# A tile of the input is made 128 bytes wider, and every tile behind it in SBUF moves by 128 bytes

## The chip, the core and the metric

The kernel runs on one core of a Trainium2 chip. The metric is device time in microseconds (us) of one execution. The core has five engines that run side by side: TensorE (PE in the profile, its weight loads PEld), VectorE (DVE), ScalarE (ACT), GpSimd (POOL) and SyncE (SP), which here issues nearly all the DMAs. Tiles lie in SBUF, 128 partitions wide. A tile has the same start address in each partition, and "offset" below is that address modulo 512 bytes.

## What is computed

Tokens (2 sequences of 4096, 192 wide) pass a causal convolution of 7 taps whose weights are a softmax per head, then a gated layer, then a second layer with ELU:

```python
w = softmax(weight)                                  # 8 heads x 7 taps
x = einsum('hk,bskhg->bshg', w, unfold(x))           # (8192, 192)
gate = 1.0 / (1.0 + np.exp(-(x @ w_gate)))           # 192 -> 1536
x = (gate * (x @ w_val)) @ w_out                     # 1536 -> 192
h = x @ w_in                                         # 192 -> 2048
g = np.where(h > 0.0, h, np.exp(np.minimum(h, 0.0)) - 1.0)
return g @ w_out2                                    # 2048 -> 192
```

## The kernel before

The 8192 tokens are cut into 16 blocks of 512 (`TB`). Each float32 operand of a product is split into a high and a low part (`h`, `l`, type fp32r), and a product is the sum of three matmuls: high by high, low by high, high by low. All large matmuls come from one helper, `mm` on L294: 64 partitions of weights by 128 columns, times 64 partitions by 512 tokens. They stand in pairs, one for the lower 64 partitions and one for the upper (`HALVES`), and each one has a weight load of its own.

- `front` (L294 with output `ps`) makes one 128-wide piece of a layer's hidden width from the block's tiles `xn`, `xs`, `xr` (the first 128 rows, the same with its halves exchanged, and the remaining 64 rows held twice). Weights: `w1h`, `w1l` in the first layer, `w3h`, `w3l` in the second.
- ACT and DVE evaluate the gate or the ELU (L311, L313, L323 to L327), ACT copies the result to `gh` (L334), and DVE writes the rest into `gl` (L340).
- `back` (L294 with output `a`) multiplies `gh` and `gl` with `w2s` or `w4s`, two steps later (`LAG`).
- `exchange` (L150, L151) makes `xs` from `xn` by two DMAs within SBUF. `end1` and `end2` fold the sums into the next layer's `xn`, `xs`, `xr` or write the output; their `three` is made from `two` by DMA (L399, L400, L445).
- `load_x` (L153) fetches a block of x from HBM into a tile `x0` or `x1`, 518 floats wide: 512 tokens and 6 before them (`PAD`). `conv` makes the convolution from it, on TensorE for two of its parts (L172, weights in the tiles `gh` and `gl`, whole 128 partitions, float32), on DVE for the others (L179, L183).
- Weights come from HBM as 64-bit numbers in the first 200 us and are split by `narrow` into the resident tiles.

The order of the work is written out by hand: a list of steps, with `CONV`, `PREPARED` and `at` to say at which step a piece of side work is issued. The changed line touches none of these.

Where tiles lie. SBUF is given out pool by pool, in the order in which the pools are opened, and within a pool in the order in which its tiles are first asked for; each tile is rounded up to 32 bytes. The built program of before has these addresses (bytes within a partition):

| tiles | first address | offset in 512 | read by matmuls as |
|---|---|---|---|
| `w1h`, `w1l`, `w3h`, `w3l`, `w2s`, `w4s` | 16,512 to 96,384 | 128, all of them | weights, in pieces of 512 bytes |
| `x0`, two buffers | 148,896 and 150,976 | 416 and 448 | moving operand of L172 |
| `x1`, one buffer | 153,056 | 480 | moving operand of L172 |
| `xcv`, `xn`, `xs`, `xr` | 155,136 to 192,000 | 0 | moving operand of `front` |
| `g`, `e`, `gh`, `gl`, `one`, `two` | 196,096 to 226,816 | 0 | `gh`, `gl`: moving operand of `back`, weights of L172 |

Of the kernel before, what the change touches and what calls it, by code (L numbers as in the profile page):

```python
# [8 lines left out]
F32 = mybir.dt.float32  # L9
# [11 lines left out]
P = 128  # L21
DR = D - P
TB = 512
NB = B * S // TB
PAD = TAPS - 1
# [33 lines left out]
def conv_glu_elu_kernel(  # L59
# [23 lines left out]
    xin = ctx.enter_context(tc.tile_pool(name="xin", bufs=2))  # L83
# [53 lines left out]
    xin_t = {}  # L137
# [14 lines left out]

    def load_x(b, i):  # L153

        t = xin_t[b, i] = xin.tile([P, TB + PAD], F32, tag=f"x{i}", name=f"x{i}", bufs=2 - i)
        if i == 0:
            bi, t0 = divmod(b * TB, S)
            nc.sync.dma_start(t, xp[0:P, bi, t0:t0 + TB + PAD])
        else:
            for h in range(2):  # L160
                bi, t0 = divmod((b + h) * TB, S)
                (nc.sync if b else nc.scalar).dma_start(t[DR * h:DR * (h + 1)], xp[P:D, bi, t0:t0 + TB + PAD])
        yield

    def conv(b, i):


        x = xin_t[b, i]
        if (b, i) in diagonals:
            acc = ps_w.tile([P, TB], F32, tag="w", name="ps")  # L170
            for k, w in enumerate(diagonals[b, i]):
                nc.tensor.matmul(acc, w, x[:, k:k + TB], start=k == 0, stop=k == TAPS - 1)  # L172
            yield
        else:
            acc = xcv.tile([P, TB], F32, tag=f"xcv{i}", name="xcv")
            for k in range(TAPS):
                w, xk = cwn[:, i, k:k + 1], x[:, k:k + TB]
                if k:
                    nc.vector.scalar_tensor_tensor(acc, xk, w, acc, ALU.mult, ALU.add)  # L179
                elif b == 2:  # L180
                    nc.scalar.mul(acc, xk, w)
                else:
                    nc.vector.tensor_scalar_mul(acc, xk, w)  # L183
                yield

        for blocks in ([0], [1]) if i and b == 2 else ([0, 1], ) if i else ([0], ):
            rows = [slice(DR * n, DR * (n + 1)) if i else slice(0, P) for n in blocks]
            made = [parts(1, b + n, "nr"[i]) for n in blocks]
            for (h, l), r in zip(made, rows):
                nc.scalar.copy(h[r], acc[r])  # L190
            yield
            for (h, l), r in zip(made, rows):
                nc.vector.tensor_sub(l[r], acc[r], f32(h[r]))
            if i == 0:
                exchange(1, b)
            yield
            if i:
                for n, r in zip(blocks, rows):
                    t = f32(parts_t[1, b + n]["r"])
                    nc.sync.dma_start(t[DR * (1 - n):DR * (2 - n)], t[r])  # L200
                yield
# [279 lines left out]
    with tc.manual_schedule():  # L481
# [28 lines left out]

        nc.sync.dma_start(cws, cw)
        next(load_x(0, 0))
        next(load_x(0, 1))
        next(jobs[0])
        next(load_x(1, 0))
        next(jobs[1])
        next(jobs[2])
# [34 lines left out]
        for (b, i), pieces in CONV.items():  # L552
            f = conv(b, i)
# [8 lines left out]
        for i in range(int(min(extra)) - 1, len(steps) + LAG + 2):  # L562
# [3 lines left out]
            if past and past[0][1] < 2:  # L566
                kind, b, j = past[0]
                past = [(kind, n, j) for n in range(2)] if b else []
            if now:
                kind, b, j = now  # L570
# [77 lines left out]
```

## Time and profile before

| | |
|---|---|
| Time, median of 3 runs | 1227.03 us (1226.5 to 1228.39) |
| Span of the profiled execution, first to last instruction | 1224.6 us |
| PE busy | 1215.9 us, 99% |
| PEld busy | 1037.0 us, 85% |
| DVE, ACT, POOL busy | 848.6, 791.3, 77.0 us |
| Granted TensorE clock | 9 (90% or more) in all 40 slices |

The page gives engine totals first, then the span in slices, then the chain of work that ended last. A matmul's own duration in the trace is its time from start to the end of its drain, which overlaps the next one; what a stream of matmuls costs is read from the distance between starts. "Pair" below means the two matmuls of the two halves, which start within some nanoseconds of each other in most of the trace.

### The profile page before, as it was taken

The numbers are of one execution on the slowest core, as the hardware profiler recorded it, in microseconds if no ns is written. First come the engines' busy times: TensorE is split into PE (matmuls) and PEld (weight loads), VectorE is DVE, ScalarE is ACT, GpSimd is POOL, SyncE is SP. The second block draws the span as 40 slices with busy tenths as digits, with TensorE's granted clock in tenths as the row PEclk, the third lists the DMA queues.
The fourth block names the chain that finished last, engine by engine and source line by source line (L and its number), as shares of the span: only waits on it lengthen the run. The fifth ranks groups of instructions, "written<-read, shape, count | busy, mean of one in ns | idle before, by whom it ended". The sixth has DMA issues, their size and how long they took to land.

```text
span 1224.6 us, 24965 instructions
## 1 busy us (share of the span) xinstructions
PE 1215.9 (99%) x10276; PEld 1037.0 (85%) x10276; DVE 848.6 (69%) x1288; ACT 791.3 (65%) x1376; POOL 77.0 (6%) x66
## 2 busy tenths in 40 slices
PE   9999999999999999999999999999999999999998
PEld 5889999888888888887888899999888888888886
DVE  8997698785447876577666676666766667664565
ACT  5555788854448885448854488445884468844686
POOL 0000000101001000011001010010100100001010
PEclk9999999999999999999999999999999999999999
DMA  6655340311001020111112011020110201111100
GB/s 156 220 194 177 104 134 27 87 53 44 9 19 44 18 61 20 31 30 45 29 34 56 7 44 45 18 61 1 44 44 19 61 11 35 44 35 27 27 14 18
DMA packets 31954, 65.78 MB, mean 54 GB/s; under 512 B 4512, under 2 KB 15776, under 8 KB 31840
## 3 DMA queue, kind: packets, MB, share of 16 engines
q1 hardware_dynamic: 31680, 63.92, 18.7%
q8 instruction: 80, 1.31, 0.4%
q10 hardware_dynamic: 160, 0.27, 0.1%
q14 instruction: 34, 0.28, 0.1%
HBM read 19.74 MB, written 6.29 MB: 21 GB/s over the span
## 4 chain that ended last, share of the span: by engine, by line
PE 92%; DVE 3%; ACT 2%; issue 1%; DMA 1%; SPq 1%; ACTq 0%; DVEq 0%
PE ps L294 51%; PE a L294 41%; DMA s<-in_w_dram 1%; ACT e L324 0%; DVE g L327 0%; ACT e L323 0%; SPq L216 0%; DVE gl L340 0%; ACT gh L334 0%; DVE h L249 0%; DVE g L313 0%; ACT gh L133 0%; DVE xcv L179 0%; ACT t L236 0%; DVE t L243 0%
## 5 line engine op out<-in xcount | busy, mean ns | idle before, releaser
L334 ACT CAST gh<-g 128x512 fp32r<-128x512 f32 x448 | 273.7, 618 | 187.7 <-DVE g L313 145.8
L340 DVE TENSOR_TENSOR gl<-g,gh 128x512 fp32r<-128x512 f32 x448 | 332.4, 755 | 77.0 <-ACT gh L334 66.7
L294 PE MATMUL a<-gh,w4s 64*128 64x512 f32 x1536 | 275.8, 393 | 0.1
L327 DVE SCALAR_TENSOR_TENSOR g<-e,ps 128x512 f32<-128x512 f32 x256 | 174.5, 687 | 123.2 <-ACT e L324 122.3
L313 DVE TENSOR_TENSOR g<-e,ps 128x512 f32<-128x512 f32 x192 | 131.7, 686 | 152.1 <-ACT e L311 146.0
L311 ACT ACTIVATE e<-ps 128x512 f32<-128x512 f32 x192 | 114.8, 598 | 179.3 <-PE ps L294 177.8
L294 PE MATMUL a<-gl,w4s 64*128 64x512 f32 x1024 | 218.2, 392 | 0.2 <-DVE gl L340 0.2
L294 PE MATMUL a<-gh,w2s 64*128 64x512 f32 x1152 | 214.9, 392 | 0.0
L294 PEld LDWEIGHTS a<-gh,w4s 64*128 64x128 f32 x1536 | 163.9, 185 | 26.4 <-DVE one L391 1.8
L294 PE MATMUL a<-gl,w2s 64*128 64x512 f32 x768 | 170.3, 392 | 1.8 <-DVE gl L340 1.8
L294 PE MATMUL ps<-xn,w1h 64*128 64x512 f32 x768 | 170.0, 392 | 0.4 <-DVE g L313 0.4
L294 PE MATMUL ps<-xs,w1h 64*128 64x512 f32 x768 | 169.2, 392 | 0.3 <-DMA xs<-xn 0.3
L294 PE MATMUL ps<-xr,w1h 64*128 64x512 f32 x768 | 168.5, 391 | 0.0
L323 ACT ACTIVATE e<-ps 128x512 f32<-128x512 f32 x256 | 150.8, 589 | 25.5 <-PE ps L294 25.0
L324 ACT ACTIVATE e<-e 128x512 f32<-128x512 f32 x256 | 161.9, 633 | 8.1
L294 PEld LDWEIGHTS a<-gh,w2s 64*128 64x128 f32 x1152 | 131.9, 185 | 18.0
L294 PEld LDWEIGHTS a<-gl,w4s 64*128 64x128 f32 x1024 | 115.0, 185 | 17.0 <-DVE gl L340 1.2
L294 PE MATMUL ps<-xn,w3h 64*128 64x512 f32 x512 | 111.1, 392 | 0.4 <-DVE g L327 0.2
L294 PE MATMUL ps<-xs,w3h 64*128 64x512 f32 x512 | 110.1, 391 | 0.0
L294 PE MATMUL ps<-xr,w3h 64*128 64x512 f32 x512 | 109.9, 391 | 0.0
L294 PEld LDWEIGHTS a<-gl,w2s 64*128 64x128 f32 x768 | 93.5, 185 | 14.5 <-DVE gl L340 3.0
L294 PEld LDWEIGHTS ps<-xn,w1h 64*128 64x128 f32 x768 | 92.2, 185 | 14.9 <-DVE g L313 1.7
(99 smaller groups left out, 1513.1 us busy)
## 6 DMA issues: line engine op xcount, KB each, us to landing
xs<-xn SPq DMA_DIRECT2D x64, 256.0 KB, 3.7
m<-s SPq DMA_DIRECT2D x14, 767.8 KB, 3.7
s<-in_w_dram SPq DMA_DIRECT2D x57, 128.0 KB, 2.9
three<-two SPq DMA_DIRECT2D x47, 128.0 KB, 2.2
s<-in_w_dram SPq DMA_DIRECT2D x6, 768.0 KB, 4.6
x<-in_xp_dram SPq DMA_DIRECT2D x16, 259.0 KB, 3.8
xr<-xr SPq DMA_DIRECT2D x16, 256.0 KB, 3.4
out_dram<-one SPq DMA_DIRECT2D x16, 256.0 KB, 2.0
```

Source lines behind the costliest of these rows:

```text
L294: return nc.tensor.matmul(ps, w, x, start=first, stop=last)
L311: nc.scalar.activation(s, gate, AF.Sigmoid)
L313: nc.vector.tensor_mul(g, s, val)
L323: nc.scalar.activation(e, h, AF.Relu, scale=-1.0)
L324: nc.scalar.activation(e, e, AF.Exp, scale=-1.0)
L327: nc.vector.scalar_tensor_tensor(g, e, -1.0, h, ALU.add, ALU.max)
L334: nc.scalar.copy(gh, g)
L340: nc.vector.tensor_sub(gl, g, f32(gh))
```

## The change

`load_x` asks for a tile that is 32 floats (128 bytes) wider where `i` is 1, and uses its first 518 columns, so that the tile `x1` (one buffer) takes 128 bytes more. The DMAs and the convolution read and write what they did. All tiles that are given out behind `x1` move up by 128 bytes: `xcv`, `xn`, `xs`, `xr`, `g`, `e`, `gh`, `gl`, `one`, `two` go from offset 0 to offset 128. The weights, `x0`, `x1` and the staging tiles of `narrow` stay where they were. In the built program each engine has the same instructions in the same order, with the same waits.

```diff
     def load_x(b, i):
 
-        t = xin_t[b, i] = xin.tile([P, TB + PAD], F32, tag=f"x{i}", name=f"x{i}", bufs=2 - i)
+
+
+        t = xin.tile([P, TB + PAD + 32 * i], F32, tag=f"x{i}", name=f"x{i}", bufs=2 - i)
+        t = xin_t[b, i] = t[:, 0:TB + PAD]
         if i == 0:
```

## Rows read from the trace of the kernel before

**Rows 1.** The page: span, busy us and share by engine, clock in 40 slices.

```profile
span 1224.6 us, 24965 instructions
...
PE 1215.9 (99%) x10276; PEld 1037.0 (85%) x10276; DVE 848.6 (69%) x1288; ACT 791.3 (65%) x1376; POOL 77.0 (6%) x66
...
PEclk9999999999999999999999999999999999999999
```

**Rows 2.** The page: the chain that ended last, its shares by engine.

```profile
PE 92%; DVE 3%; ACT 2%; issue 1%; DMA 1%; SPq 1%; ACTq 0%; DVEq 0%
```

**Rows 3.** Stretches, L294 alone: stretch, its us, busy us (instructions), clock, DMA.

```profile
0.00:1224.60 1224.60, 1197.91 (x10240) 1029.59 (x10240) 1.00 0.19 54
...
300.00:500.00 200.00, 200.00 (x1723) 164.29 (x1721) 1.00 0.12 30
580.00:700.00 120.00, 120.00 (x1032) 96.59 (x1030) 1.00 0.13 32
```

**Rows 4.** Timeline of PE: start us, us, instruction, xcount merged, idle before.

```profile
399.96 0.40 PE L294 MATMUL ps<-xr,w3l 64*128 64x512 f32 x2
400.20 0.40 PE L294 MATMUL ps<-xr,w3h 64*128 64x512 f32 x2
400.43 0.63 PE L294 MATMUL a<-gh,w4s 64*128 64x512 f32 x4
400.89 0.40 PE L294 MATMUL a<-gl,w4s 64*128 64x512 f32 x2
```

**Rows 5.** Timeline of PEld, the same stretch.

```profile
399.96 0.19 PEld L294 LDWEIGHTS ps<-xr,w3h 64*128 64x128 f32 x2
400.20 0.42 PEld L294 LDWEIGHTS a<-gh,w4s 64*128 64x128 f32 x4
```

**Rows 6.** Timeline of PE, the convolution's matmuls of the first 18 us.

```profile
6.22 3.60 PE L172 MATMUL ps<-x,gh 128*128 128x512 f32 x8
9.66 2.74 PE L172 MATMUL ps<-x,gl 128*128 128x512 f32 x6
12.23 3.60 PE L172 MATMUL ps<-x,gh 128*128 128x512 f32 x8
```

**Rows 7.** Timeline of PE behind its longest stall.

```profile
50.53 0.50 PE L294 MATMUL a<-gl,w2s 64*128 64x512 f32 x2 [1.64 <-DVE gl L340]
50.87 0.39 PE L294 MATMUL a<-gh,w2s 64*128 64x512 f32 x2
51.10 0.39 PE L294 MATMUL a<-gl,w2s 64*128 64x512 f32 x2
51.33 0.62 PE L294 MATMUL a<-gh,w2s 64*128 64x512 f32 x4
51.79 0.40 PE L294 MATMUL a<-gl,w2s 64*128 64x512 f32 x2
```

**Rows 8.** The convolution's tile `xcv`: duration ns min/median/max, by line.

```profile
L179 DVE SCALAR_TENSOR_TENSOR xcv<-x,cwn,xcv x132: 739/746/753, 6.1 to 1091.2; 128x512 f32<-128x512 f32 x132
```

**Rows 9.** What L294 waited for in the whole span, us and times.

```profile
  DVE gl L340: 6.3, 9
  DVE g L327: 2.3, 6
  DVE g L313: 2.0, 5
  DVE one L391: 1.8, 6
  DMA xs<-xn: 1.0, 2
```

**Rows 10.** DMA issues on the page: xcount, KB each, us to landing.

```profile
xs<-xn SPq DMA_DIRECT2D x64, 256.0 KB, 3.7
...
x<-in_xp_dram SPq DMA_DIRECT2D x16, 259.0 KB, 3.8
```

## The prediction

> **What bounds the kernel now.** The page comes first [rows 1]: PE is busy for 1215.9 of 1224.6 us, and the clock is at its upper level in every slice. The chain of work that ended last says the same [rows 2]: 92% of it is PE. What the matmuls waited for is small: the five largest entries of that list add up to 13.4 us [rows 9], nearly all in the first 225 us and at changes of block groups. So this kernel has one large number: the distance between one pair of matmuls and the next. The stretches of L294 alone give it [rows 3]. There are 10,240 matmuls, 5,120 pairs, in 1197.9 us of busy time: 234.0 ns a pair, with the drains in front of stalls. In an undisturbed stretch it is purer. Between 300 and 500 us 1,723 matmuls touch the window. About 3.4 of them began before it (a matmul lasts 0.40 us, two start every 0.23 us), so (1723 - 3.4) / 2 = 860 pairs in 200 us: 232.6 ns. Between 580 and 700 us it is 514 pairs in 120 us: 233.3 ns.
>
> Is that the least that a pair can take? 512 columns at one per period of 2.4 GHz are 213.3 ns. The convolution's float32 matmuls show what surrounds such a stream [rows 6]: from 6.22 to 12.23 us there are 14 passes (8 and 6), 429.3 ns each. That is 1030 periods, which I read as 512 columns at two periods, and 6 periods (2.6 ns) of overhead. One period a column and the same overhead would be 215.9 ns. A pair of L294 takes 16.7 ns more than that, 7%, and over 5,120 pairs that is **85 us** whose cause no row names.
>
> Three causes can be ruled out. It is not the clock (1.00 in these stretches, [rows 3]). It is not waiting for weights: the load for the next pair starts with the present pair, at 399.96 us, lasts 0.19 us and is done at 400.15, while that pair starts at 400.20 [rows 4, 5]. It is not the supply of instructions: after a stall of 1.64 us, in which a queue can fill, and one long first step, the pairs go at 0.23 us again at once [rows 7]. Two candidates are left. One is a fixed cost of two half-height matmuls side by side. The other is that the weight load's reads of SBUF and the moving operand's reads, which run together for 0.19 of the 0.23 us, now and then get in each other's way. In favour of the second, the distance isn't constant: the same kinds of instructions go at 232.6 ns in one stretch and at 233.3 in another [rows 3], with nothing waited for.
>
> **The change, part by part.** *The wider tile itself* adds no instruction and no byte to any transfer; 128 bytes of each partition are given away and the last tile still fits. Cost: nothing.
>
> *Vector, scalar and GpSimd work on tiles that moved.* The nearest row is the convolution on DVE, whose input starts at seven addresses, four bytes apart, from offsets 416, 448 and 480: 132 instructions lie between 739 and 753 ns [rows 8]. So a start address is worth at most 14 ns there, 2%. Even 2% on all of DVE's 848.6 us would fit into its idle 376 us; where PE does wait for DVE and ACT (12.4 of the 13.4 us above), 2% is 0.2 us. I take 0, and ±0.3 us for the range.
>
> *DMAs within SBUF.* `xs<-xn` (64 of them, 3.7 us to landing) now starts from and lands at offset 128 instead of 0. Landings at odd places are on the page already: the loads of x go to offsets 416 and 448, from HBM, and land in 3.8 us [rows 10]. PE waited for `xs` twice, 1.0 us in all [rows 9]; the rest is covered by the hand-written order, which issues these exchanges steps ahead. I take 0; a landing 0.3 us later would add at most 0.3 us at each of the two places that show a wait. [...]
>
> *The pairs.* Weights start at offset 128 for every load. The moving operands of L294 started at 0, so each load began 128 bytes ahead of the stream beside it (the same piece of 512 bytes); after the change both begin at 128. It is the only relation between the two reads that the change alters, and it alters it for all 5,120 pairs. Its price is bounded by the excess on the good side: 16.7 ns, 85 us. The only variation of the distance that rows show without a wait is 0.7 ns, 3.6 us. On the bad side nothing bounds it but the same size by symmetry. I take a fifth of the excess, 3.3 ns a pair, as an estimate between 0.7 and 16.7, nearer to what has been seen: 5,120 x 3.3 ns = 17 us. The sign is the weaker part. For a gain speaks that the load starts with the pair, and the stream, which reads four times as many bytes in about the same time, has to overtake a load that begins ahead of it; from one common start it needn't overtake. Against it: from a common start both first reads are in the same place.
>
> **Sum.** Span 1224.6 - 17 = 1207.6 us. The timed median is 2.4 us above the span of the profiled execution, and I keep that: **1210 us**.
>
> **The rivals.**
>
> *No change.* The excess is the fixed cost of the two half-height matmuls, or depends on addresses only below 128 bytes; then the time is 1227 us, within 2.5 (the two distances of 232.6 and 233.3 may change their shares: 0.7 ns on a quarter of the pairs is 0.9 us). For it: in the convolution, weights at offset 0 and moving operand at 448 to 504 run with 2.6 ns of overhead, so the overlap of a load alone costs nothing there [rows 6]; but that stream reads at half the rate. [...]
>
> *Much faster.* All of the excess is such interference, and a common start ends it: 5,120 x 16.7 = 85 us, 1142 us. For it: the load lasts 0.19 of 0.23 us, so there is room for it to be all. Against: the two reads keep running together whatever the offset.
>
> *Slower.* The place is L294 again. If reads collide when both are in the same part of a 512-byte piece, the head start of 128 bytes is what has kept them apart at each start, and the change takes it away. The same 3.3 ns with the other sign give 1244 us; the excess doubled gives 1312. It decides from 0.5 ns a pair on, that is 2.5 us: a distance above 233.1 ns between 300 and 500 us.
>
> **How the numbers follow.** A step of 0.2% (2.5 us) is about what measurements of this kernel can tell from no change. Faster by part of the excess (centre 1210): 0.35. Much faster (1142): 0.12. No change: 0.33. Slower: 0.20. So faster is 0.47, same 0.33, slower 0.20. The range runs from 1185 (half of the excess gone: 42 us) to 1245 (the forecast's size with the other sign, and 1 us of the small terms). It leaves out the far end of the gain, about 0.11, and the larger losses, about 0.09. Cases of both signs hold the chances, so the forecast's own range stands beside it: 1190 to 1224.
>
> **What would show it.** Right: in the stretch 300 to 500 us the count of L294 rises from 1,723 to about 1,748 (229.3 ns a pair), the load rows keep their 0.19 us, waits stay as in [rows 9], and DVE's and ACT's durations stay. No change: 1,723 again, within 4. Slower: below 1,718. Wrong in another way: a new wait of PE on `xs` or `gl`, which would mean that the moved transfers or DVE's writes have become the late ones, or a clock below 1.00 in some stretch. If the pairs' distance stays and the time moves, none of the above holds.

## The result: 1200.43 us, 2.2% less, and where it shows

The changed kernel takes 1200.43 us (median of 4 runs, 1200.16 to 1200.80) against 1227.09 us for the kernel before (4 runs, 1226.5 to 1228.39): a ratio of 0.9779, 95% interval 0.9765 to 0.9793. The forecast was 1210 us with a range of 1185 to 1245.

The page of the changed kernel, in the form of [rows 1]:

```profile
span 1198.8 us, 24965 instructions
...
PE 1188.4 (99%) x10276; PEld 1071.5 (89%) x10276; DVE 845.9 (71%) x1288; ACT 789.2 (66%) x1376; POOL 77.2 (6%) x66
...
PEclk9999999999999999999999999999999999999999
```

The span is 25.8 us shorter, with the same instructions and the same clock; PE is still busy for 99% of it. So PE's stream itself has become denser. The helper `mm` stands on L297 now. Its stretches, with the columns of [rows 3]:

```profile
0.00:1198.80 1198.80, 1170.68 (x10240) 1064.08 (x10240) 1.00 0.20 55
...
300.00:500.00 200.00, 200.00 (x1765) 164.87 (x1763) 1.00 0.12 30
580.00:700.00 120.00, 120.00 (x1059) 118.64 (x1057) 1.00 0.15 37
```

10,240 matmuls are busy for 27.2 us less than before. Between 300 and 500 us 1,765 of them touch the window instead of 1,723. A window without a change of block groups is the cleaner measure, and the following stretch of L297 serves as the yardstick from here on:

```profile
240.00:340.00 100.00, 100.00 (x886) 82.62 (x884) 1.00 0.15 38
```

(886 - 3.4) / 2 = 441.3 pairs in 100 us, **226.6 ns a pair** (3.4 is the prediction's estimate of the matmuls that began before the window). The kernel before, in the same window:

```profile
240.00:340.00 100.00, 100.00 (x864) 82.74 (x862) 1.00 0.15 38
```

That is 430.3 pairs, 232.4 ns. The timeline of PE and of PEld in the changed kernel answers to [rows 4, 5]:

```profile
399.58 0.39 PE L297 MATMUL a<-gl,w4s 64*128 64x512 f32 x2
399.81 0.39 PE L297 MATMUL a<-gh,w4s 64*128 64x512 f32 x2
400.03 0.39 PE L297 MATMUL a<-gl,w4s 64*128 64x512 f32 x2
400.26 0.62 PE L297 MATMUL a<-gh,w4s 64*128 64x512 f32 x4
```

```profile
399.81 0.19 PEld L297 LDWEIGHTS a<-gl,w4s 64*128 64x128 f32 x2
400.04 0.41 PEld L297 LDWEIGHTS a<-gh,w4s 64*128 64x128 f32 x4
```

A load takes 0.19 us, as before; only the distance from pair to pair has fallen, to 0.22 and 0.23 us by turns. (That PEld is busy for 118.64 of 120 us between 580 and 700 us doesn't mean longer loads. In that stretch one half starts some 0.10 us behind the other, so the two loads of a pair, 0.18 us each, overlap less. The distance of the pairs is 226.7 ns there too.)

5.8 ns on 5,120 pairs are 29.7 us, of which 27.2 show in PE's busy time (which counts the whole 0.39 us of a matmul in front of a stall) and 25.8 in the span. The rest went where a faster engine waits more. What L297, its matmuls and its weight loads, waited for, against [rows 9]:

```profile
  DVE gl L343: 8.2, 10
  DVE g L330: 3.2, 7
  DVE one L394: 2.7, 7
  DVE g L316: 2.3, 4
  DVE w1l L266: 1.1, 3
  DMA xs<-xn: 0.9, 2
```

The same five entries as in [rows 9] come to 17.3 us instead of 13.4: in the first 225 us and at the changes of groups, PE now comes earlier to the results of DVE.

### The profile page after: what moved, and what is told of

The parts are those of the page before. It is cut to its first block, busy times and chain, and to the rows that moved or that the text cites. A ratio compares the mean times of both kernels' runs of the same rounds, so it can differ in the third digit from the quotient of the medians.

```text
span 1198.8 us, 24965 instructions
## 1 busy us (share of the span) xinstructions
PE 1188.4 (99%) x10276; PEld 1071.5 (89%) x10276; DVE 845.9 (71%) x1288; ACT 789.2 (66%) x1376; POOL 77.2 (6%) x66
## 4 chain that ended last, share of the span: by engine, by line
PE 90%; DVE 5%; ACT 2%; issue 1%; DMA 1%; SPq 0%; ACTq 0%; DVEq 0%
PE ps L297 50%; PE a L297 40%; DVE gl L343 1%; DVE g L316 1%; DMA m<-s 1%; DVE h L252 1%; DVE g L330 0%; ACT e L327 0%; ACT e L326 0%; DVE t L248 0%; DVE w1l L266 0%; SPq L219 0%; DVE t L246 0%; DVE t L254 0%; DVE xcv L182 0%
## 5 line engine op out<-in xcount | busy, mean ns | idle before, releaser
L297 PE MATMUL a<-gh,w4s 64*128 64x512 f32 x1536 | 281.1, 388 | 0.3 <-ACT one L391 0.2
L297 PE MATMUL a<-gl,w4s 64*128 64x512 f32 x1024 | 225.5, 387 | 0.2 <-DVE gl L343 0.2
L297 PE MATMUL a<-gh,w2s 64*128 64x512 f32 x1152 | 219.0, 387 | 0.0
L297 PEld LDWEIGHTS a<-gh,w4s 64*128 64x128 f32 x1536 | 178.2, 184 | 17.6 <-DVE one L394 2.7
L297 PE MATMUL a<-gl,w2s 64*128 64x512 f32 x768 | 175.9, 387 | 2.6 <-DVE gl L343 2.6
L297 PE MATMUL ps<-xn,w1h 64*128 64x512 f32 x768 | 175.9, 387 | 0.6 <-DVE g L316 0.5
L297 PE MATMUL ps<-xs,w1h 64*128 64x512 f32 x768 | 174.5, 386 | 0.2 <-DMA xs<-xn 0.2
L297 PE MATMUL ps<-xr,w1h 64*128 64x512 f32 x768 | 174.5, 386 | 0.0
L297 PEld LDWEIGHTS a<-gh,w2s 64*128 64x128 f32 x1152 | 142.5, 184 | 10.8
L297 PEld LDWEIGHTS a<-gl,w4s 64*128 64x128 f32 x1024 | 127.0, 184 | 10.6 <-DVE gl L343 1.2
L297 PE MATMUL ps<-xn,w3h 64*128 64x512 f32 x512 | 114.8, 388 | 0.6 <-DVE g L330 0.4
L297 PEld LDWEIGHTS a<-gl,w2s 64*128 64x128 f32 x768 | 103.4, 184 | 11.6 <-DVE gl L343 4.2
L297 PE MATMUL ps<-xr,w3h 64*128 64x512 f32 x512 | 113.3, 386 | 0.0
L297 PE MATMUL ps<-xs,w3h 64*128 64x512 f32 x512 | 113.3, 386 | 0.0
L297 PEld LDWEIGHTS ps<-xn,w1h 64*128 64x128 f32 x768 | 102.7, 184 | 9.9 <-DVE g L316 1.8
```

The costliest lines, as they stand in the source:

```text
L297: return nc.tensor.matmul(ps, w, x, start=first, stop=last)
```

## Experiments: what about the 128 bytes matters

"Relation" below is the weights' start minus the moving operand's start. Three theories were set against each other. A: the relation of the two reads decides. B: the moving operand's own place decides. C: the matmuls' reads have nothing to do with it, and it is the writes and transfers of other engines into the moved tiles.

### e1: streams of extra matmuls, one for each relation

```diff
+        flat = w4s.rearrange("p j c m -> p (j c m)")
+        nc.vector.memset(f32(flat[:, 0:2 * 768]), 0.5)
...
+        for k in range(2 * N): nc.tensor.matmul((pl, pu)[k % 2], flat[HALVES[k % 2], 648:648 + P],
+            flat[HALVES[k % 2], 0:0 + TB], start=k < 2, stop=k >= 2 * N - 2)
...
```

> The kernel before, with streams of extra matmuls ahead of its work that nothing uses (so its time means nothing): each stream is 48 pairs like those of the large matmuls, both operands from one scratch area, and the streams differ in where the weights start relative to the moving operand: 0, 32, 64 ... 480 bytes within 512, then 4 and 16 bytes, then relations 0, 128, 256 and 0 again with both operands moved by 128, 128, 256 and 384 bytes. After them 48 full-height matmuls (128 partitions) and 48 of the lower half alone, each at relations 0, 128, 256, 384. Theory A (the relation of the two reads within 512 bytes decides): 226.7 ns a pair at relation 0 and 232.5 to 233.4 at 128, wherever both lie. Theory B (the moving operand's own place decides): all streams with the moving operand in one place are alike, within 0.3 ns; those moved by 256 differ from them. Theory C (the matmuls' reads have nothing to do with it, but the writes and transfers of other engines into the moved tiles): all alike, and moved ones too. The full-height and single-half streams tell what the remaining 10.8 ns above 215.9 are: if they belong to two half-height matmuls side by side, a single stream takes 215.9 ns at relation 0; if they belong to the load beside the stream, it takes 226.7.

The timeline of PE in this kernel, one row for a stream: L529 has relation 0, L530 32, L537 256, L538 288, L547 0 with both operands 128 bytes on, L548 then 128; L553 is full-height (whole 128 partitions) at 256 and L554 at 384, L557 and L558 the same for the lower half alone.

```profile
6.90 11.54 PE L529 MATMUL ps<-w4s 64*128 64x512 f32 x96
18.27 11.37 PE L530 MATMUL ps<-w4s 64*128 64x512 f32 x96
...
96.44 11.06 PE L537 MATMUL ps<-w4s 64*128 64x512 f32 x96
107.33 11.37 PE L538 MATMUL ps<-w4s 64*128 64x512 f32 x96
...
207.87 11.08 PE L547 MATMUL ps<-w4s 64*128 64x512 f32 x96
218.78 11.33 PE L548 MATMUL ps<-w4s 64*128 64x512 f32 x96
...
274.03 11.05 PE L553 MATMUL ps<-w4s 128*128 128x512 f32 x48
284.92 11.32 PE L554 MATMUL ps<-w4s 128*128 128x512 f32 x48
...
318.35 11.05 PE L557 MATMUL ps<-w4s 64*128 64x512 f32 x48
329.24 11.32 PE L558 MATMUL ps<-w4s 64*128 64x512 f32 x48
```

Take the 0.39 us of its last matmul off a row and divide by 47 steps: 227 ns at relations 0 and 256, 233 or 234 at the others. (L529 and others begin with some longer steps.) From the tenth start of each stream to its last but one, the mean distance in ns is:

| relation | 0 | 32 | 64 | 96 | 128 | 160 | 192 | 224 |
|---|---|---|---|---|---|---|---|---|
| pairs | 226.7 | 233.3 | 233.3 | 234.3 | 232.6 | 233.5 | 228.8 | 233.4 |
| relation + 256 | 226.7 | 233.3 | 233.3 | 234.3 | 232.6 | 233.4 | 228.8 | 233.4 |

Relations 4 and 16 took 232.4 and 233.3. With both operands moved on, relation 0 took 226.65 at places 128 and 384, relation 256 took 226.8 at place 256, relation 128 took 232.3 at place 128. The full-height matmuls took 226.7, 232.3, 226.7, 232.3 at relations 0, 128, 256, 384, and the lower half alone the same four numbers. So theory A holds and B and C fall. From 18 to 340 us, through all streams but the first, DVE, ACT and POOL are busy for 0.00 us, so nothing else runs that could tell the relations apart. Two more things follow. The pattern repeats every **256** bytes, not 512. And nothing of it belongs to the two half-height matmuls side by side, since one matmul at a time behaves the same (226.7 and 232.3 ns).

### e2, e3, e9, e5: the whole kernel at other places

Four layouts separate relation and place. e2 and e5 give `x1` another width; e3 and e9 put 128 bytes ahead of the weights as well.

```diff
-        t = xin.tile([P, TB + PAD + 32 * i], F32, tag=f"x{i}", name=f"x{i}", bufs=2 - i)
+        t = xin.tile([P, TB + PAD + 64 * i], F32, tag=f"x{i}", name=f"x{i}", bufs=2 - i)   # e2; e5: 96 * i
```

```diff
+    const.tile([P, 32], F32, name="gap")            # e3 (with x1 as before), e9 (with x1 as after)
     w1 = [const.tile([P, J1, 3, P], F32R, name=f"w1{c}") for c in "hl"]
```

> The tile x1 is 256 bytes wider in place of 128: moving operands at offset 256, weights at 128, so the load begins 128 bytes behind the stream's start (relation 384). Theory A: another distance than at relations 0 and 128, no number known beforehand; if equality alone is good, 232 ns or more and 1227 us or more. Theory B (own place, repeating every 256 bytes): as before, 1227 us. Any shift helps: 1200 us.

> The kernel before with 128 bytes given away ahead of the weights: weights at 256, moving operands at 128, as after the change, but the relation is 128, as before. Theory A: 232.6 ns a pair and 1227 us. Theory B: 226.7 ns and 1200 us. Theory C: 1200 us, since the activations lie where they lie after the change.

> The change, and 128 bytes more given away ahead of the weights: weights and moving operands both at offset 256, relation 0 as after the change, but x0, x1 and the staging tiles move too. Theory A: 226.7 ns a pair and 1200 us. If the place of the moving operand (128 after the change) had any part in it: as with moving operands at 256 and weights at 128, 1228 us.

> The tile x1 is 384 bytes wider: moving operands at offset 384, weights at 128, relation 256. By the sweep of extra streams (226.65 ns at relation 256, as at 0) what counts repeats every 256 bytes: 226.7 ns a pair and 1200 us. If equality within 512 bytes were what counts, as the change's own words have it: 232 to 233 ns and 1227 us.

| kernel | weights | moving | relation | time, us | ratio to before, interval |
|---|---|---|---|---|---|
| before | 128 | 0 | 128 | 1227.1 | |
| after | 128 | 128 | 0 | 1200.4 | 0.9779, 0.9765 to 0.9793 |
| e2 | 128 | 256 | -128 (384) | 1228.2 | 1.0006, 0.9996 to 1.0015 |
| e3 | 256 | 128 | 128 | 1228.0 | 1.0002, 0.9993 to 1.0012 |
| e9 | 256 | 256 | 0 | 1200.8 | 0.9781, 0.9765 to 0.9798 |
| e5 | 128 | 384 | -256 (256) | 1200.6 | 0.9781, 0.9766 to 0.9795 |

Each ratio is to runs of the kernel before that were made beside it; their medians lie between 1227.0 and 1227.7 us.

e3 is the sharpest of them: every tile behind `x1` lies exactly where it lies after the change, and nothing is gained, because the weights moved along. e9 moves those tiles by 128 bytes more and leaves the weights where e3 has them, and the gain is there again. e5 shows in the whole kernel that 256 is as good as 0, and e2 that 384 is as bad as 128. Offsets modulo 512, as they are given ahead of the prediction, are finer than need be: modulo 256 is enough.

### e4: only the second products moved

The 128 bytes are given away behind `xn`, `xs`, `xr`, so that only `gh` and `gl` (and `g`, `e`, `one`, `two`) move; `x1` has its old width.

```diff
+    gap = ctx.enter_context(tc.tile_pool(name="gap", bufs=1))
     ew = ctx.enter_context(tc.tile_pool(name="ew", bufs=2))
...
+    gap.tile([P, 32], F32, name="gap")
     w1 = [const.tile([P, J1, 3, P], F32R, name=f"w1{c}") for c in "hl"]
```

> The 128 bytes are given away behind xn, xs, xr instead of ahead of them: the moving operands of the second product of each layer (gh, gl) go to offset 128, those of the first (xn, xs, xr) stay at 0. Theories A and B: 226.7 ns in stretches of gh and gl, 232.5 where xn, xs, xr stream; 4480 of 10240 matmuls, 2240 pairs x 5.9 ns = 13 us less than before, 1214 us. Theory C by transfers (xs, three): 1227 us; by writes of gh, gl: 1200 us, with no difference between the two kinds of pairs.

It took 1222.4 us, 0.9959 (0.9945 to 0.9973): a gain of 5.1 us, two fifths of the 13 us that theory A was credited with. The timeline of PE shows why. In the first layer, five pairs of `a` stand between nine of `ps`; in the second, ten:

```profile
300.29 0.59 PE L299 MATMUL ps<-xn,w1h 64*128 64x512 f32 x2
...
302.39 0.83 PE L299 MATMUL a<-gh,w2s 64*128 64x512 f32 x4
...
303.55 0.59 PE L299 MATMUL ps<-xn,w1h 64*128 64x512 f32 x2
```

```profile
400.46 0.67 PE L299 MATMUL a<-gh,w4s 64*128 64x512 f32 x4
...
401.62 0.66 PE L299 MATMUL a<-gh,w4s 64*128 64x512 f32 x4
...
402.75 0.43 PE L299 MATMUL ps<-xn,w3h 64*128 64x512 f32 x2
...
404.85 0.67 PE L299 MATMUL a<-gh,w4s 64*128 64x512 f32 x4
```

From 300.29 to 302.39 us nine pairs of the first product take 2.10 us, 233.3 ns each; the next five, at relation 0, take 1.16 us, 232.0 ns each: almost no gain. In the second layer ten pairs at relation 0 take 2.29 us, 229.0 ns each: the first five, from 400.46 to 401.62 us, 232.0 ns each as in the first layer, the last five, to 402.75 us, 226.0 by these rounded rows. (Over all such groups behind 230 us, the sixth to tenth pair take 226.7 to 227.0 ns each.) So here a stream needs about five pairs at relation 0 before it runs at 226.7 ns. 1,280 pairs of the second layer at 3.6 ns less than 232.6 make 4.6 us, which is most of what the run gained. The changed kernel shows the same settling behind its longest stall, the counterpart of [rows 7]:

```profile
50.94 0.50 PE L297 MATMUL a<-gl,w2s 64*128 64x512 f32 x2 [2.30 <-DVE gl L343]
51.28 0.39 PE L297 MATMUL a<-gh,w2s 64*128 64x512 f32 x2
...
52.89 0.39 PE L297 MATMUL ps<-xn,w1h 64*128 64x512 f32 x2
...
54.93 0.40 PE L297 MATMUL ps<-xn,w1h 64*128 64x512 f32 x2
```

From 51.28 to 52.89 us seven pairs take 230.0 ns each; from 52.89 to 54.93 nine take 226.7. How many pairs it takes differs: in e1, the stream of relation 256 at L537 had this pace from its first step, the one at L549 from its eleventh.

### e6 and e7: relations that aren't 0, and the other sign

```diff
-        t = xin.tile([P, TB + PAD + 32 * i], F32, tag=f"x{i}", name=f"x{i}", bufs=2 - i)
+        t = xin.tile([P, TB + PAD + 48 * i], F32, tag=f"x{i}", name=f"x{i}", bufs=2 - i)   # e6; e7: 8 * i
```

> The tile x1 is 192 bytes wider: moving operands at 192, weights at 128, relation 448. The extra streams took 228.81 ns there, 3.8 ns less than at 128: 5120 x 3.8 = 19 us below the kernel before, 1208 us. If a gain needs exact equality within 256 bytes: 1227 us.

> The tile x1 is 32 bytes wider: moving operands at 32, weights at 128, relation 96. The extra streams took 234.32 ns there, 1.7 ns more than at 128: 5120 x 1.7 = 9 us above the kernel before, 1236 us. If offsets that differ are all alike: 1227 us.

e7 took 1233.5 us, 1.0049 (1.0034 to 1.0064): slower than before, by 6.5 us where 9 were expected. Its stretch of L297 shows why:

```profile
240.00:340.00 100.00, 100.00 (x858) 80.32 (x856) 1.00 0.14 35
```

That is 234.0 ns a pair by the same working, against 232.4 before. The same kind of padding can lose as well as win. e6 took 1217.4 us, 0.9905 (0.9874 to 0.9935), between the two expectations, with single runs from 1211.4 to 1218.6. Its stretches of L297:

```profile
240.00:340.00 100.00, 100.00 (x876) 81.98 (x876) 1.00 0.15 38
580.00:680.00 100.00, 100.00 (x860) 81.59 (x858) 1.00 0.16 38
```

229.2 ns in one stretch and 233.5 in another of the same execution (228.9 and 233.3 from start to start): at this relation a stream can keep either pace. In the kernel before, the pace goes over at stalls, from 232.4 to 233.3 ns near 558 us and back near 857; so the 232.6 and 233.3 ns of [rows 3] are the same thing there. But a stall is not needed. In e6 the pace goes over to 233.3 near 1016 us, and between 996.5 and 1100 us PE and PEld wait for nothing. The trace of e3 shows that the two halves even keep paces of their own:

```profile
574.58 0.43 PE L295 MATMUL a<-gh,w4s 64*128 64x512 f32 x2
...
614.32 0.58 PE L295 MATMUL a<-gh,w4s 64*128 64x512 f32 x2
```

Such a row is one matmul of 0.39 us and the lag of the second half behind the first, and the lag grows by 0.15 us in 39.7 us. Between 572 and 616 us one half starts every 232.4 ns and the other every 233.3. Different shares of the two paces would account for the spread of e6's runs; only one of them has a trace, so this is not shown. At relations 0 and 256 every undisturbed stretch behind 230 us of the three kernels (the changed one, e9, e5) ran at 226.7.

### e10: every relation in steps of four bytes

The edit is that of e1, with 64 streams of the lower half.

> The kernel before, with 64 streams of extra matmuls ahead of its work that nothing uses (its time means nothing): 40 matmuls of the lower 64 partitions each, relation 0, 4, 8 ... 252 bytes. If relations other than 0 were alike, 232 to 233 ns for all 63. If collisions come with particular distances: a spread between 228 and 235 ns, as the coarse streams had, with 226.7 at 0. A relation below 226.7 would be a layout better than the change's.

```profile
6.90 9.74 PE L529 MATMUL ps<-w4s 64*128 64x512 f32 x40
...
387.71 9.66 PE L570 MATMUL ps<-w4s 64*128 64x512 f32 x40
...
592.26 9.23 PE L592 MATMUL ps<-w4s 64*128 64x512 f32 x40
```

Relation 0 (L529) settled at 226.7 ns after some longer first steps. The other 63 lay between 226.7 and 237.6 ns (relation 164, L570). Seven of them, relations 100, 120, 132, 144, 156, 228 and 252 (L592), also ran at 226.7; each was tried once, right behind another stream, so whether these relations would hold that pace from another start is open, and e6 warns against it. None was below 226.7: among these 64 relations none is better than the change's.

### e8: smaller weights, fewer moving columns

The edit is that of e1, for the lower half alone, with other sizes.

> The kernel before, with streams of extra matmuls ahead of its work that nothing uses (its time means nothing): 48 matmuls of the lower 64 partitions each, at relations 0 and 128; first with 512 moving columns and weights of 32, 64, 96 and 128 columns, then with weights of 128 columns and 128, 256 and 384 moving columns. At relation 0 a full matmul takes 226.7 ns, which is 544 periods of 2.4 GHz, 32 more than its 512 columns. If the load beside the stream costs a quarter of a period for each of its 128 columns: 520, 528, 536, 544 periods, so 216.7, 220.0, 223.3 and 226.7 ns; if each load costs the same whatever its size: 226.7 for all four. With 256 and 384 moving columns: 288 and 416 periods (120.0 and 173.3 ns) by the first, unless the load itself, 0.19 us in the trace, is the longer one. At relation 128 the loss against relation 0 (5.8 ns at full size) shrinks with the weights' columns if it is collisions of the two reads.

```profile
6.90 11.46 PE L529 MATMUL ps<-w4s 64*32 64x512 f32 x48
...
29.29 11.20 PE L531 MATMUL ps<-w4s 64*64 64x512 f32 x48
...
73.49 11.05 PE L535 MATMUL ps<-w4s 64*128 64x512 f32 x48
84.38 11.32 PE L536 MATMUL ps<-w4s 64*128 64x512 f32 x48
```

Rows of relation 0 for weights of 32, 64 and 128 columns, then relation 128. The theory of a quarter period a column falls: smaller loads are not cheaper, but dearer (231.7 ns with 32 columns, 229.9 with 64, 230.1 with 96, 226.7 with 128). At relation 128 the first three took 230.5, 229.2 and 231.8, so with these the relation makes no clear difference. The second half of this run can't be compared with the first. Its streams begin at 95.5 us with 128 moving columns, and during the first of them the granted clock fell to the lower level. In the stretch from 92 to 140 us, all engines, PEld is busy for 47.24 of 48 us and the mean granted clock is 0.58:

```profile
92.00:140.00 48.00, 48.00 (x231) 47.24 (x231) 0.00 (x0) 0.00 (x0) 0.00 (x0) 0.58 0.00 1
```

At the lower level 256 and 384 columns took 213.3 and 320.0 ns, 0.833 ns a column, at relation 0 and at 128 alike. The trace of the kernel before has that level as 0.50, from 1224.3 to 1224.6 us, behind its last matmul; the mean of 0.58 fits a fall to 0.50 near 99.7 us. Scaled by 0.50, a column takes 0.417 ns at the full clock, which is one per period of 2.4 GHz, and 512 columns take 213.3 ns: an estimate from these two traces.

### e11: other types

The edit is again that of e1, full-height, on bf16 and float32 views of the scratch area.

> The kernel before, with streams of 48 extra full-height matmuls each ahead of its work that nothing uses (its time means nothing): bf16 at relations 0, 4, 32, 64, 96, 128 and 192 bytes, then float32 at 0, 32, 96, 128 and 192, then fp32r at 0 and 128. Weights of 128 columns and 512 moving columns throughout. If the clash is of two reads of SBUF as such, bf16 (half the bytes a column) shows it too, with a smaller loss than the 5.8 ns of fp32r; if it needs the full byte rate of fp32r (four bytes a column at one period a column), bf16 takes 213 to 216 ns at every relation. The convolution's float32 passes took 429.3 ns at relations other than 0, with nothing to gain: 429.3 at all five. fp32r as in the other streams, 226.7 and 232.3.

The timeline of PE; L530 to L536 are bf16 at seven relations, L537 to L541 float32 at five, L542 and L543 fp32r at 0 and 128:

```profile
17.39 10.52 PE L531 MATMUL ps<-w4s 128*128 128x512 bf16 x48
27.75 10.52 PE L532 MATMUL ps<-w4s 128*128 128x512 bf16 x48
...
120.75 41.36 PE L538 MATMUL ps<-w4s 128*128 128x512 f32 x96
161.95 41.36 PE L539 MATMUL ps<-w4s 128*128 128x512 f32 x96
...
285.15 11.50 PE L542 MATMUL ps<-w4s 128*128 128x512 f32 x48
296.49 11.32 PE L543 MATMUL ps<-w4s 128*128 128x512 f32 x48
```

bf16 takes 215.8 ns at every relation (10.36 us from L531 to L532, 48 matmuls), float32 429.2 ns a pass at every relation (41.20 us, 96 passes), fp32r 226.7 and 232.3. So of these three types only fp32r shows the clash. There the load's place changes the running matmul's pace by 5.6 ns. fp32r is also the only one with four bytes a column at 0.44 ns a column (226.7 ns for 512; bf16 has two bytes a column and takes 0.42 ns, float32 four bytes and 0.84 ns). That this rate is the reason is a guess that fits; no run changes the rate alone.

## Why the prediction was right, point by point

*The bound.* Right. PE's pair distance was the one large number, and all of the gain lies in it.

*The excess.* The 215.9 ns that the prediction built from the float32 passes of [rows 6] is what bf16 streams take (215.8, e11). The 213.3 ns underneath it, 512 columns at one per period of 2.4 GHz, agree with the estimate from e8 (0.833 ns a column at a granted clock of 0.50). So fp32r did carry 16.7 ns of excess. The prediction named two causes. A fixed cost of two half-height matmuls is refuted: one matmul at a time has the same pace, 226.7 and 232.3 ns at relations 0 and 128 (e1). Interference of the load with the stream beside it is what the relation shows, for 5.8 of the 16.7 ns: only the load reads the weights' address, and moving that address alone changes the pace, from 226.7 ns at relation 0 to 232.6 at 128 (e1). What the other 10.9 ns are stays open.

*The size.* The term that was mis-sized is the 3.3 ns a pair, "a fifth of the excess". It was 5.8 ns, 35% of it: 29.7 us in place of 17. No row gave the fifth; it was a choice between 0.7 and 16.7 ns, and that it came within a factor of two is luck. The result lies inside the forecast's own range of 1190 to 1224, nearer to its low side. The "much faster" rival, all of the excess gone, did not come: 10.9 ns stay at relation 0.

*The sign, right for a wrong reason.* The prediction argued that a load with a head start of 128 bytes has to be overtaken. If that were it, a load that begins 128 bytes behind would do no harm and one 256 bytes ahead would do more. The runs show the contrary: relation 384, 128 bytes behind, is as bad as 128 (1228.2 us against 1227.1, e2), and 256 is as good as 0 (226.7 ns at both in e1, 1200.6 us against 1200.4 in e5). So the sign was luck as well.

*No change.* This rival needed a fixed cost, or a pattern that repeats within 128 bytes; neither holds for the 5.8 ns (e1). Its support from the convolution's passes was set aside because they run at half the rate, rightly: float32 takes 429.2 ns a pass at all five relations (e11).

*Slower.* This rival said that reads collide when both are in the same part of a piece, and that the head start kept them apart. It is refuted: at relation 0, where both begin in the same place, the pace is 226.7 ns, and no relation has a lower one (e1, e10). A loss by moving tiles does exist, 6.5 us at relation 96 (e7), but not by that mechanism.

*Small terms.* DVE's convolution kept its time (745 ns in the middle, 746 in [rows 8]). `xs<-xn` lands in 3.6 us, 3.7 in [rows 10], though it now starts and ends at offset 128, and PE's two waits for `xs` come to 0.9 us, 1.0 in [rows 9]. So no run shows the landing 0.3 us later that stands in the 1 us of small terms of the prediction's range.

*What the sum left out.* The waits were to stay as in [rows 9]. They grew by 3.9 us, nearly all of it for DVE, so that the span gained 25.8 of 29.7 us. The wait for `gl` rose from 6.3 to 8.2 us, and the prediction took a new wait of that kind for a sign that DVE's writes come late; but DVE was not slower (845.9 us busy, 848.6 before), so PE comes earlier.

## What to carry to other kernels

When a stream of matmuls is dense, compare its start-to-start distance with that of a stream of another type over the same columns (here 232.6 ns in fp32r against 215.8 in bf16); a steady excess that no wait explains is worth a test of its own. For fp32r matmuls with a load beside each, place weights and moving operands a multiple of 256 bytes apart (here 226.7 ns a pair instead of 232.6, worth 2.2% of the kernel), and look at the addresses again whenever a tile ahead of them changes its size. A stream of dummy matmuls ahead of the kernel's own work measures such a thing for dozens of layouts in one run.

## What the runs showed of the hardware that was not expected

- The pace of fp32r matmuls with loads beside them depends on where the weights lie relative to the moving operand, modulo 256 bytes: 226.7 ns at 0, 228.3 to 237.6 at most other relations, with four bytes enough to lose it (232.4 ns at relation 4 in e1). bf16 and float32 streams show nothing of it (215.8 and 429.2 ns at every relation tried, e11).
- Where the relation isn't 0, a stream can hold more than one pace (e6: 229.2 and 233.5 ns), go from one to the other without a stall, and the two halves can hold different ones at the same time (e3: 232.4 and 233.3 ns). At relation 0 it can take several pairs to settle (about five in e4, none to ten in e1).
- 226.7 ns are 10.9 more than bf16's 215.8 (e11). What these 10.9 ns are is open: narrower loads did not reduce them (229.9 to 231.7 ns at relation 0, e8), and no stream was tried without loads. Why the pattern has 256 bytes is open too; no run looks inside the memory.
